# Gates multiplied into the experts' outputs instead of their inputs, and token rows stored unscaled

## The chip, the cores and the metric

The kernel runs on one core of a Trainium2 chip. The metric is the time of one execution in microseconds of the device, median of several runs. Engines are TensorE (PE; PEld for its weight loads), VectorE (DVE), ScalarE (ACT), GpSimd (POOL) and SyncE (SP), whose queue issues most of the transfers.

## The reference

Three computations follow one another. The first is a linear attention over 4 batches, 8 heads, 768 steps and heads of 48, in float32:

```
state = alpha_t[:, None] * state + k_t v_t^T        # per batch and head
y_t   = q_t state
```

The 3072 tokens of 384 features that come out go to a mixture of 8 experts, one expert per token:

```
logits = (x / (|x| + 1e-6)) @ (emb / (|emb| + 1e-6)).T / tau
e      = argmax(logits);  gate = softmax(logits)[e]
out    = gate * (relu(x @ w1[e]) @ w2[e])            # 384 -> 1024 -> 384
```

A dense block ends it: `h = x @ w_in` (2048 wide), `g = h if h > 0 else exp(min(h, 0)) - 1`, `g @ w_out`.

## The kernel before

**Attention and router.** The 3072 tokens are 24 tiles of 128 (6 pieces of the sequence by 4 batches). A loop written out by hand, `fast()`, goes through them one tile per iteration, and an `ending()` takes the last two; inside, the order of instructions on each engine is the order of the text (a manual schedule). For tile i, VectorE scans the decays (`stR`, L354, and `stA`, L364), GpSimd multiplies keys and queries by them (`Kh` L357, `Qh` L366), TensorE makes the scores psS (L394), VectorE masks them (L401), TensorE makes the outputs psY (L421, L439) and the state update, and one more TensorE product, psX (L476), gives the token rows, head by head in their final order, and the router's logits. `stD` copies the rows from PSUM (L493) and sums their squares (L495).

**Router groups.** Tiles are taken in groups, `GROUPS` (L38): 0–5, 6–11, 12–15, 16–19, 20–21, 22–23. When a group's last tile is done, `stR1` (L523 and following, VectorE) picks the expert of every token, `stR2` counts on TensorE (L572 to L576) where each token comes in its expert's region, and `stX` and `gates` make the gate. Of expert e the region in DRAM is `xs[e*REG:]`.

**Putting rows.** `scale_x` (L587) multiplies a tile's rows by their gates on ScalarE (L594) and splits the 32-bit words into two 16-bit planes (L601 on ScalarE, L603 on VectorE or GpSimd). `put` (L614, L615) adds the token's number and scatters the 128 rows to `xs` by an indirect DMA, issued by GpSimd. A DMA transpose (L263) brings an expert's rows back with features on the partitions, and `join` (L277 ScalarE, L279 GpSimd or VectorE) makes 32-bit words of the two planes again.

**Expert 0 starts before its last rows are stored.** Tiles 20 to 23 do not wait for the scatter and the transpose: `column` (L899) makes for each of them a matrix, gate where a token's place equals the column and zero elsewhere, and fp32 matmuls (L912) bring the rows to their columns in PSUM; three more (L938) add the joined rows of the other tiles by an identity matrix.

**Experts.** `moe1` goes through 8 experts of at most `CAPS` tokens, 432 down to 368. Every fp32 product is made of three fp32r passes, of high and low parts: `mm1` (L1064 to L1066), Relu and split (L1068 ScalarE, L1069 VectorE), `mm2` one or more blocks later (L1094 to L1096). Beside it, the weights of later experts are loaded by SP and split (L191 ScalarE, L194 VectorE); weights of the dense block are rounded by L229 to L235 on three engines; the next expert's rows are joined on GpSimd at f-step f−2 and split (`turn`, L1084 ScalarE, L1085 VectorE) at f−4. At the end of an expert its three output blocks go from PSUM to `x2T` (L1101, L1103 on ScalarE, L1102 on VectorE). `moe2` is the dense block; it writes the token's rows back by indirect DMA.

**Startup.** SP issues the loads of the first tiles, then `cs` (L709, the constants, among them `tok`, the tokens' numbers, and `base`), then more tiles. GpSimd's order there is: masks and zeros, the memsets of `vt` (L718), `Kh` and `Qh` of tile 0, of tile 1, the memsets of `G`. Twenty warm-up matmuls on TensorE stand ahead of the first psS:

```
                warm(ps1, "psY", 20)
                nc.vector.memset(pz[:, 0:1], A_FLOOR)
                nc.vector.memset(cum[:, 0], 0.0)
                for t in vt:
                    nc.gpsimd.memset(t[:, NP * CW:], 0.0)
                zero = xp.tile([128, 1, XW], U16, tag="xt", name="zero")
                for j in range(2):
                    stR(j); stA(j); stH(j); stE(j)
```

Of the kernel before, what the change touches and what calls it, by code (L numbers as in the profile page):

```python
# [8 lines left out]
F32 = mybir.dt.float32  # L9
# [28 lines left out]
GROUPS = [list(range(6)), list(range(6, 12)), list(range(12, 16)), list(range(16, 20)), [20, 21], [22, 23]]  # L38
NMID = 9
# [3 lines left out]
LOWS = (15, 18)  # L43
PAIRS = (15, 18, 19)
# [8 lines left out]
XW = 2 * (DM + 1)  # L53
# [14 lines left out]
def fused_kernel(ctx, tc, qk, a, v, w12, wi, wo, cst, cols, out):  # L68
# [9 lines left out]
    idl = dram.tile([N + CAP, 2], U16, name="idl")  # L78

# [9 lines left out]
    ident16 = const.tile([128, 128], BF16, name="ident16")  # L89
    base16 = const.tile([128, 1, E], BF16, name="base16")  # L90
# [5 lines left out]
    idf = const.tile([128, NT], F32, name="idf")  # L96
# [13 lines left out]
    tick = const.tile([1, 1], F32, name="tick")  # L110

# [161 lines left out]
    def join(eng, t, planes, kk, n):  # L273

        dst, src = words(t[:, :n]), planes[:, 2 * kk:2 * kk + 2, :n]
# [11 lines left out]
    def attention():  # L287
        with ExitStack() as st:
# [4 lines left out]
            xp = st.enter_context(tc.tile_pool(name="xp", bufs=14))  # L293
# [80 lines left out]
            def stT(i):  # L374
                if i < NT - B:
                    t = ps1.tile([128, NP, C2], F32, name="psT")
# [92 lines left out]
            def stD(i, keep=False):  # L469
# [13 lines left out]
                if keep:  # L483
                    late.pop()()
                rows = x[:, :, :CW]
                xi = xp.tile([128, XW], U16, name="xt")
                x3 = xi[:, :2 * DM].bitcast(F32).rearrange("p (n d) -> p n d", n=NP)
                sq = wk.tile([128, NP, CW], BF16, bufs=1, tag="junk", name="sq")
                if keep:
                    px[i] = x3  # L490
                else:
                    xt[i] = xi
                    nc.scalar.activation(out=x3, in_=rows, func=AF.Copy)  # L493
                    rows = x3
                nc.scalar.activation(out=sq, in_=rows, func=AF.Square, accum_out=ss[:, i:i + 1])  # L495
                if keep:
                    nc.scalar.activation(out=x3, in_=rows, func=AF.Copy)
# [51 lines left out]
            def gates(g):  # L549
                gt = gate[g]  # L550
                return [
                    lambda: nc.vector.tensor_scalar(gt, gt, 1e-9, None, op0=ALU.add),
                    lambda: nc.vector.reciprocal(gt, gt),
                ]

            def count_tile(g):
# [5 lines left out]
                if g == NG - 2:  # L562
                    return ps1.tile([128, 8, E], F32, tag="psT", name="psR")
                return psD.tile([128, 8, E], F32, tag="psX", name="psR")

            def stR2(g):
# [5 lines left out]
                nc.tensor.matmul(r, ident16, base16.to_broadcast(s3), start=True, stop=False)  # L572
                nc.tensor.matmul(r, ones16, cum[:, g:g + 1].to_broadcast(s3), start=False, stop=False)
# [12 lines left out]
            scaled = {}  # L586

# [802 lines left out]
```

## Time and profile before

| | us |
|---|---|
| median of 3 runs (780.39 to 780.43) | 780.4 |
| the profiled execution | 781.37 |
| its span in the trace | 779.7 |
| TensorE busy in the span | 759.2 (97%) |
| VectorE, ScalarE, GpSimd busy | 543.7, 355.1, 243.1 |
| mean granted clock of TensorE, of full | 0.988 |

The span runs from the first recorded instruction to the last; the execution's own time has 1.7 us more around it. A row of the timeline gives start and length of an instruction (or of several alike, with their count), its engine and line, what it writes from what, and in brackets how long the engine was idle before it and what it then waited for. A row of the windows gives for one stretch the busy time of every engine with the number of its instructions, the granted clock of TensorE as a share of 2.4 GHz, and the use of the DMA engines.

### The profile page before, as it was taken

The numbers are of one execution on the slowest core, as the hardware profiler recorded it, in microseconds if no ns is written. First come the engines' busy times: TensorE is split into PE (matmuls) and PEld (weight loads), VectorE is DVE, ScalarE is ACT, GpSimd is POOL, SyncE is SP. The second block draws the span as 40 slices with busy tenths as digits, with TensorE's granted clock in tenths as the row PEclk, the third lists the DMA queues.
The fourth block names the chain that finished last, engine by engine and source line by source line (L and its number), as shares of the span: only waits on it lengthen the run. The fifth ranks groups of instructions, "written<-read, shape, count | busy, mean of one in ns | idle before, by whom it ended". The sixth has DMA issues, their size and how long they took to land.

```text
span 779.7 us, 13453 instructions
## 1 busy us (share of the span) xinstructions
PE 759.2 (97%) x4982; PEld 689.5 (88%) x4982; DVE 543.7 (70%) x976; ACT 355.1 (46%) x698; POOL 243.1 (31%) x298
## 2 busy tenths in 40 slices
PE   8999998899999999999999999999999999999996
PEld 4888887489999999999887999999999999999996
DVE  7898998648999999995767745455454545545442
ACT  2557886635455555554545433333332333333331
POOL 7758787433565566451000020020010002002002
PEclk9999998899999999999999999999999999999998
DMA  9999952547757776751000010010000001001001
GB/s 194 249 258 254 253 155 75 164 119 187 216 188 215 234 205 211 216 181 32 1 1 1 0 42 1 1 41 0 1 11 31 0 1 42 1 0 42 1 1 41
DMA packets 59652, 75.31 MB, mean 97 GB/s; under 512 B 31134, under 2 KB 36126, under 8 KB 59582
## 3 DMA queue, kind: packets, MB, share of 16 engines
q1 hardware_dynamic: 56510, 64.97, 31.3%
q0 software_dynamic: 3072, 9.45, 3.4%
q8 instruction: 39, 0.64, 0.4%
q14 instruction: 31, 0.25, 0.1%
HBM read 57.20 MB, written 12.22 MB: 89 GB/s over the span
## 4 chain that ended last, share of the span: by engine, by line
issue 32%; PE 32%; DVE 8%; POOL 3%; ACT 3%; DMA 1%; POOLq 0%; ACTq 0%; SPq 0%; DVEq 0%
PE h L1243 6%; PE y L1095 3%; PE h L1065 3%; PE h L1066 3%; PE y L1096 3%; PE h L1064 3%; PE y L1094 3%; POOL out_dram L1277 2%; PE o L1266 2%; PE o L1264 2%; PE o L1265 2%; DVE wlo L194 2%; DVE dlo L250 1%; DVE hl L1069 1%; DVE g L1249 1%
## 5 line engine op out<-in xcount | busy, mean ns | idle before, releaser
L1245 DVE TENSOR_SCALAR mn<-h 128x512 f32<-128x512 f32 x96 | 66.3, 690 | 139.6 <-PE h L1243 139.6
L1246 ACT ACTIVATE mn<-mn 128x512 f32<-128x512 f32 x96 | 60.8, 633 | 171.6 <-DVE mn L1245 171.6
L1266 PE MATMUL o<-dwo,gl 128*128 128x384 f32 x384 | 129.6, 338 | 1.6 <-DVE gl L1253 1.6
L1265 PE MATMUL o<-dlo,gh 128*128 128x384 f32 x384 | 128.4, 334 | 0.0
L1277 POOL DMA_INDIRECT out_dram<-ob,ids x24 | 23.7, 988 | 335.5 <-ACT ob L1274 331.9
L1264 PE MATMUL o<-dwo,gh 128*128 128x384 f32 x384 | 128.3, 334 | 0.0
L1243 PE MATMUL h<-xh,dlo 128*128 128x512 f32 x288 | 113.1, 393 | 0.0
L1243 PE MATMUL h<-xl,dwi 128*128 128x512 f32 x288 | 112.9, 392 | 0.0
L1243 PE MATMUL h<-xh,dwi 128*128 128x512 f32 x288 | 112.7, 391 | 0.0
L1252 ACT ACTIVATE gh<-g 128x512 fp32r<-128x512 f32 x96 | 60.7, 633 | 77.6 <-DVE g L1249 77.6
L194 DVE TENSOR_TENSOR wlo<-raw,whi 128x512 fp32r<-128x512 f32 x96 | 88.1, 942 | 1.3 <-ACT whi L191 1.2
L1249 DVE SCALAR_TENSOR_TENSOR g<-mn,h 128x512 f32<-128x512 f32 x96 | 66.1, 689 | 15.3 <-ACT mn L1246 14.9
L1264 PEld LDWEIGHTS o<-dwo,gh 128*128 128x128 f32 x384 | 72.0, 187 | 4.2
L1265 PEld LDWEIGHTS o<-dlo,gh 128*128 128x128 f32 x384 | 72.0, 187 | 4.0
L1266 PEld LDWEIGHTS o<-dwo,gl 128*128 128x128 f32 x384 | 72.2, 188 | 2.7 <-DVE gl L1253 2.0
L1068 ACT ACTIVATE hh<-h 128x432 fp32r<-128x432 f32 (+6 forms) x64 | 32.4, 506 | 81.4 <-PE h L1066 76.8
L1095 PE MATMUL y<-hl,whi 128*128 128x432 f32 (+6 forms) x192 | 66.8, 348 | 1.4 <-DVE hl L1069 1.4
L1064 PE MATMUL h<-xh,whi 128*128 128x432 f32 (+6 forms) x192 | 66.5, 347 | 0.7 <-ACTq L1113 0.7
L1065 PE MATMUL h<-xl,whi 128*128 128x432 f32 (+6 forms) x192 | 66.4, 346 | 0.2 <-DVEq L1113 0.2
L1253 DVE TENSOR_TENSOR gl<-g,gh 128x512 fp32r<-128x512 f32 x96 | 65.6, 684 | 1.1 <-ACT gh L1252 1.1
L1066 PE MATMUL h<-xh,wlo 128*128 128x432 f32 (+6 forms) x192 | 66.4, 346 | 0.0
L1094 PE MATMUL y<-hh,whi 128*128 128x432 f32 (+6 forms) x192 | 66.3, 346 | 0.0
(228 smaller groups left out, 1484.5 us busy)
## 6 DMA issues: line engine op xcount, KB each, us to landing
raw<-in_w_dram SPq DMA_DIRECT2D x96, 256.0 KB, 3.4
qk<-in_qk_dram SPq DMA_DIRECT2D x46, 192.0 KB, 5.7
raw<-in_wi_dram SPq DMA_DIRECT2D x16, 384.0 KB, 3.9
raw<-in_wo_dram SPq DMA_DIRECT2D x16, 384.0 KB, 3.8
vt<-in_v_dram SPq DMA_DIRECT2D x24, 192.0 KB, 5.8
at<-in_alpha_dram SPq DMA_DIRECT2D x40, 99.0 KB, 5.8
xs<-zero SPq DMA_DIRECT2D x7, 288.8 KB, 5.9
at<-in_alpha_dram SPq DMA_DIRECT2D x4, 231.0 KB, 4.7
```

The costliest lines, as they stand in the source:

```text
L194: nc.vector.tensor_tensor(l[:, sl], r, h[:, sl].bitcast(F32), op=ALU.subtract)
L1064: nc.tensor.matmul(ps, wh, xh[:, kk], start=(kk == 0), stop=False)
L1065: nc.tensor.matmul(ps, wh, xl[:, kk], start=False, stop=False)
L1066: nc.tensor.matmul(ps, wl, xh[:, kk], start=False, stop=(kk == KD - 1))
L1094: nc.tensor.matmul(acc[e][d], wh, hh, start=(f == 0), stop=False)
L1095: nc.tensor.matmul(acc[e][d], wh, hl, start=False, stop=False)
L1243: nc.tensor.matmul(ps, l, x, start=(n == 0), stop=(n == len(terms) - 1))
L1245: nc.vector.tensor_scalar(mn, ps, 0.0, None, op0=ALU.min)
L1249: nc.vector.scalar_tensor_tensor(g, mn, -1.0, ps, op0=ALU.add, op1=ALU.max)
L1264: nc.tensor.matmul(o_, gh[:, sl], wh, start=(f == 0), stop=False)
L1265: nc.tensor.matmul(o_, gh[:, sl], wl, start=False, stop=False)
L1266: nc.tensor.matmul(o_, gl[:, sl], wh, start=False, stop=(f == M - 1))
```

## The change

- The rows are stored without the gate. ScalarE makes the two planes straight from psX in PSUM; `scale_x` is gone. A plane now holds all 384 features (`join` and the transposed tile follow), and a row has two more words of 16 bits for its gate.
- `mark` holds the token's number and the gate of every token. A GpSimd copy at the startup fills the numbers from `cs`; `gates` writes the gates, and `put` copies both into the row.
- Each expert's gates are read from `xs` by three small SP loads (`load_g`) to a row that is the same on all partitions, and VectorE multiplies the three output blocks by it. All three evictions are VectorE's.
- Groups become 0–5, 6–11, 12–15, 16–17, 18–21, 22–23. Tiles 18 to 23 go to expert 0 by columns of 0 and 1, with their rows split into two fp32r parts (`high` by ScalarE, `low` by VectorE); 36 fp32r matmuls stand for 12 fp32 ones (24 records).
- The transpose of expert 0's rows is issued behind the put of tile 17. Its joins are one on ScalarE and two on GpSimd; the other experts' joins are on ScalarE, one f-step later than before, and so is `turn`.
- `pack` and the tests of the decays are cut into pieces that go between the first splits and matmuls of expert 0; the branch on their result is read inside the second `mm1`. `stR2` starts from `cum`, which now holds the regions' bases, so that one matmul is gone.

The core of the diff:

```diff
-GROUPS = [list(range(6)), list(range(6, 12)), list(range(12, 16)), list(range(16, 20)), [20, 21], [22, 23]]
+GROUPS = [list(range(6)), list(range(6, 12)), list(range(12, 16)), [16, 17], list(range(18, 22)), [22, 23]]
+HOT = 18
-LOWS = (15, 18)
-PAIRS = (15, 18, 19)
+LOWS = (14, 15, 16)
+PAIRS = (15, 17, 19)
-XW = 2 * (DM + 1)
+XW = 2 * (DM + 2)
...
+    mark = const.tile([128, NT, 2], F32, name="mark")
...
                 warm(ps1, "psY", 20)
+                nc.gpsimd.tensor_copy(mark[:, :, 0], c["tok"])
                 nc.vector.memset(pz[:, 0:1], A_FLOOR)
-                nc.vector.memset(cum[:, 0], 0.0)
...
-                    nc.scalar.activation(out=x3, in_=rows, func=AF.Copy)
+                def planes():
+                    nc.scalar.activation(out=xt[i][:, :2 * DM].rearrange("p (two n d) -> p two n d", two=2, n=NP),
+                                         in_=x.bitcast(U16)[:, :, :2 * CW].rearrange("p n (d two) -> p two n d", two=2), func=AF.Copy)
                 nc.scalar.activation(out=sq, in_=rows, func=AF.Square, accum_out=ss[:, i:i + 1])
+                if pz is not None and i >= HOT:
...
+                    nc.scalar.activation(out=h, in_=rows, func=AF.Copy)
+                    late.append(lambda: nc.vector.tensor_tensor(l, rows, h.bitcast(F32), op=ALU.subtract))
+                if not hold:
+                    planes()
...
-                    lambda: nc.vector.reciprocal(gt, gt),
+                    lambda: nc.vector.reciprocal(mark[:, i0:i0 + n, 1:2].rearrange("p n o -> p (n o)"), gt),
...
-                nc.gpsimd.tensor_copy(x[:, 2 * DM:].bitcast(F32), c["tok"][:, i:i + 1])
+                x = xt.pop(i)
+                nc.gpsimd.tensor_copy(x[:, 2 * DM:].bitcast(F32), mark[:, i])
...
-                    nc.vector.tensor_scalar(hot[j], num, pos[:, j:j + 1], gate[g][:, b:b + 1], op0=ALU.is_equal, op1=ALU.mult)
+                    hot[j] = wk.tile([128, CAP], F32R, tag=tag, bufs=n, name="hot")
+                    nc.vector.tensor_scalar(hot[j], num, pos[:, j:j + 1], None, op0=ALU.is_equal)
...
+                    for j in tiles:
+                        for n, t in enumerate(px[j]):
+                            nc.tensor.matmul(t0[kk], t[:, kk * 128:(kk + 1) * 128], hot[j], start=(start and j == GROUPS[g3][0] and n == 0),
+                                             stop=(stop and j == tiles[-1] and n == 1))
...
-                    join(nc.gpsimd, xj[e, kk], xr[e], kk, CAPS[e])
+                    join(nc.scalar, xj[e, kk], xr[e], kk, CAPS[e])
...
+            def load_g(e, f):
+                if f == (0 if e else EARLY):
+                    gl[e] = xj_p.tile([1, CAP], F32, tag="xj", name="gl")
+                    nc.sync.dma_start(out=gl[e][:, :CAPS[e]].rearrange("o (n u) -> o n u", u=1),
+                                      in_=xs[bass.ds(expert(e) * REG, CAPS[e]), 2 * DM + 2:].bitcast(F32).rearrange("(o n) u -> o n u", o=1))
+                if f == (2 if e else EARLY + 1):
+                    nc.sync.dma_start(out=gd[e:e + 1, :CAPS[e]], in_=gl.pop(e)[:, :CAPS[e]])
+                if f == (4 if e else 5):
+                    gs[e] = gs_p.tile([128, CAP], F32, name="gs")
+                    nc.sync.dma_start(out=gs[e][:, :CAPS[e]], in_=gd[e:e + 1, :CAPS[e]].to_broadcast([128, CAPS[e]]))
...
-                    nc.scalar.activation(out=x2T[:, 0, bass.ds(o1, n)], in_=y[0], func=AF.Copy)
-                    nc.vector.tensor_copy(x2T[:, 1, bass.ds(o2, n)], y[1])
-                    nc.scalar.activation(out=x2T[:, 2, bass.ds(o1, n)], in_=y[2], func=AF.Copy)
+                    for d in range(KD):
+                        nc.vector.tensor_tensor(x2T[:, d, bass.ds(o, n)], y[d], gt[:, :n], op=ALU.mult)
...
-                        joined(e + 1, f - 2)
-                        turn(e + 1, f - 4)
+                        joined(e + 1, f - 3)
+                        turn(e + 1, f - 5)
+                        load_g(e, f)
```

## Rows read from the trace of the kernel before

**Rows 1.** Stages in one windows answer (us, PE, PEld, DVE, ACT, POOL busy, PEclk, DMA, GB/s).
```profile
35.68:111.14 75.46, 75.46 (x1116) 67.27 (x1114) 70.64 (x163) 53.01 (x121) 55.47 (x73) 1.00 0.96 243
...
122.27:129.37 7.10, 7.10 (x57) 6.03 (x57) 6.96 (x15) 1.56 (x6) 6.26 (x10) 0.55 0.33 90
...
129.37:156.68 27.31, 23.59 (x155) 15.43 (x154) 18.62 (x106) 19.05 (x44) 13.60 (x22) 0.87 0.44 139
...
156.68:371.84 215.16, 212.85 (x1152) 207.50 (x1152) 187.57 (x283) 112.01 (x227) 105.38 (x88) 1.00 0.62 181
```

**Rows 2.** Timeline of the startup, 0 to 14 us (start, us, engine, line, tiles, [idle before <-releaser]).
```profile
3.71 0.89 SPq L336 DMA_DIRECT2D qk<-in_qk_dram  x2
...
5.73 1.26 POOL L357 TENSOR_TENSOR Kh<-qk,R 112x512 f32<-112x512 f32 x1 [1.50 <-DVE R L354]
...
6.52 0.42 SPq L709 DMA_DIRECT2D cs<-in_cst_dram  x1
...
8.56 0.33 SPq L327 DMA_DIRECT2D at<-in_alpha_dram  x1
...
8.80 1.16 PE L394 MATMUL psS<-Qh,Kh 48*128 48x128 f32 x16
...
10.16 1.29 POOL L357 TENSOR_TENSOR Kh<-qk,R 112x512 f32<-112x512 f32 x1 [1.52 <-DMA qk<-in_qk_dram]
...
12.73 1.16 PE L394 MATMUL psS<-Qh,Kh 48*128 48x128 f32 x16 [0.93 <-POOL Qh L366]
```

**Rows 3.** Timeline of the first iterations, 13.5 to 40 us.
```profile
16.33 1.25 DVE L354 TENSOR_TENSOR_SCAN R<-at,pz 112x528 f32<-112x528 f32 x1 [0.79 <-DMA at<-in_alpha_dram]
...
17.20 1.16 PE L394 MATMUL psS<-Qh,Kh 48*128 48x128 f32 x16 [0.55 <-POOL Qh L366]
...
30.34 1.16 PE L394 MATMUL psS<-Qh,Kh 48*128 48x128 f32 x16 [0.36 <-POOL Qh L366]
```

**Rows 4.** DMA issues of the whole span (xcount, KB each, median us from issue to landing).
```profile
qk<-in_qk_dram SPq DMA_DIRECT2D x4, 96.0 KB, 3.2
...
idl<-xs SPq DMA_DIRECT2D x2, 1.7 KB, 7.6
```

**Rows 5.** Timeline of the loop's last iterations, 108 to 125 us.
```profile
117.25 1.24 DVE L354 TENSOR_TENSOR_SCAN R<-at,pz 112x528 f32<-112x528 f32 x1
...
122.27 1.40 PE L394 MATMUL psS<-Qh,Kh 48*128 48x128 f32 x16 [1.87 <-POOL Qh L366]
```

**Rows 6.** VectorE's lines between 84.8 and 126 us (xcount | busy us, mean ns | idle before).
```profile
L603 DVE COPY xt<-sx 128x768 uint16<-128x768 uint16 x3 | 2.8, 936 | 0.0
...
L523 DVE TENSOR_TENSOR lg<-lg,en 128x32 f32<-128x32 f32 x1 | 1.4, 1364 | 0.0
```

**Rows 7.** Timeline of the ending, first half.
```profile
140.62 2.04 PE L476 MATMUL psX<-rhsX,yT 128*128 128x104 f32 x8 [1.69 <-ACT yT L441]
```

**Rows 8.** Timeline of the ending, second half, 142 to 165 us.
```profile
146.60 0.92 DVE L899 TENSOR_SCALAR hot<-num,pos,gt 128x432 f32<-128x432 f32 x2
...
150.08 4.62 PE L912 MATMUL t<-hot,xt 128*128 128x432 f32 x12
...
154.53 2.34 PE L938 MATMUL t<-xj,masks 128*128 128x432 f32 x6
```

**Rows 9.** Stages of single experts, the first and the third (columns as in rows 1).
```profile
161.90:190.20 28.30, 28.30 (x144) 27.07 (x145) 17.03 (x26) 12.15 (x24) 8.04 (x8) 1.00 0.72 176
...
218.00:245.00 27.00, 27.00 (x145) 26.70 (x144) 26.63 (x40) 14.89 (x31) 16.23 (x13) 1.00 0.73 223
```

**Rows 10.** Waits between 162 and 372 us (us in total, times, longest).
```profile
PEld y L1095 <- DVE hl L1069: 3.1, 5, 1.0
```

**Rows 11.** VectorE's weight subtract (L194) and output copy (L1102), 156.7 to 371.8 us.
```profile
L194 DVE TENSOR_TENSOR wlo<-raw,whi 128x512 fp32r<-128x512 f32 x87 | 81.9, 967 | 1.3 <-ACT whi L191 1.2
...
L1102 DVE COPY x2T<-y 128x432 f32 x2 | 1.2, 599 | 0.6 <-PE y L1096 0.6
```

**Rows 12.** The weight subtract between 129.4 and 156.6 us.
```profile
L194 DVE TENSOR_TENSOR wlo<-raw,whi 128x512 fp32r<-128x512 f32 x3 | 1.9, 673 | 0.0
```

More of the change, by code (lines that the diff above doesn't have):

```diff
@@ L467, in attention, with stD @@
             px = {}
[L469 removed]
+            def stD(i, soon=False, hold=False):
                 if i < 0 or i >= NT:
@@ L889, in ending @@
-                run(r2, x2 + gates(g2))
-                xr = xr_p.tile([128, 2 * KD, CAP], U16, name="xr")
-                load_rows(xr, 0, [0, KD], puts[:-1])
-                stD(i, True)
-                hot = {}
-                def column(j, tag):
-                    g, b = place[j]
-                    hot[j] = wk.tile([128, CAP], F32, tag=tag, bufs=3 if tag == "Qh" else 2, name="hot")
-                    nc.vector.tensor_scalar(hot[j], num, pos[:, j:j + 1], gate[g][:, b:b + 1], op0=ALU.is_equal, op1=ALU.mult)
@@ new lines, in ending @@
+                for j, tag in zip(GROUPS[g3], ("Kt", "Kt", "A", "A")):
+                    column(j, tag, 2)
+                run(gates(g3))
+                last = [stD(i, True, True), stD(i + 1, True, True)]
+                m1, n1 = stR1(g1)
+                t0 = [psT_p.tile([128, CAP], F32, tag="psT", name="t0")] + [psG.tile([128, CAP], F32, tag="g", name="t0") for _ in range(KD - 1)]
+                n1.pop(0)()
+                run(m1)
+                for j in GROUPS[g3][:2]:
+                    put(j)
@@ new lines, in ending @@
+                pk = pack(sm, pz[:, 192:192 + E])
+                pk.pop(0)()
+                first_x(GROUPS[g3][2:], 1)
+                first_x(GROUPS[g3], 2, True)
+                run(r1)
+                for j in GROUPS[g1]:
+                    column(j, "Kh", 2)
+                xj = []
+                for kk, eng in enumerate((nc.scalar, nc.gpsimd, nc.gpsimd)):
+                    xj.append(xj_p.tile([128, CAP], F32, tag="xj", name="xj"))
+                    join(eng, xj[kk], xr, kk, CAP)
@@ new lines, in ending @@
+                for j in GROUPS[g3][2:]:
+                    put(j)
+                run(late)
+                late.clear()
+                run(n1, dec[7:11])
+                for kk in range(KD):
+                    nc.tensor.matmul(t0[kk], c["ident"], xj[kk], start=False, stop=False)
+                run(dec[11:13])
+                for kk in range(KD):
+                    first_x(GROUPS[g1], kk, stop=True)
+                for f in last:
+                    f()
+                x1 = stX(g1)
@@ new lines, in ending, with rest_of @@
+                tests = pk[:9] + dec[13:] + pk[9:]
+                tests, rest = tests[:len(tests) - 9], tests[len(tests) - 9:]
+                run(tests[:12])
+                tests = tests[12:]
+                def rest_of(n=None):
+                    if n is not None:
+                        run(tests[:n])
+                        del tests[:n]
+                        return
+                    run(tests, x1 + gates(g1))
+                    run(rest)
+                    for j in GROUPS[g1]:
+                        put(j)
+                    load_w(2 * PIECES)
+                    split_spare(len(spare))
@@ L961, in fix @@
                             general()
-                            run(pack(sm, ps1))
+                            run(pack(sm, psT_p.tile([128, E], F32, tag="psT", name="n_ps")))
                     zero = xp.tile([128, XW], U16, tag="xt", name="zero")
```

250 lines of the change are left out of this document (91 added, 159 removed).

## The prediction

> **What bounds the kernel now.** I read the stages first, then the order of work in the stages that the change touches, then the waits of the expert stage. The stages split into two kinds. Where TensorE is full, only its own work or its clock can move the time: from 35.68 to 111.14 us it is busy 75.46 of 75.46 us, and between 156.68 and 371.84 us, the experts, 212.85 of 215.16 us [rows 1]. Where it isn't full, chains of small instructions decide: the startup, until the first psS at 8.80 us [rows 2]; the last two loop iterations, where psS waits 1.87 us for GpSimd's Qh and the granted clock is then 0.55 for 7.10 us [rows 1, 5]; and the ending, from psS of tile 23 at 129.37 to the first expert matmul at 156.68, 27.31 us with 23.59 busy [rows 1]. The dense second product behind 371.84 us is not changed but for which rows it stores, and I cost it at nothing: TensorE sets its pace and its stores are issued by GpSimd beside it.
>
> The sum is made against the profiled execution, 781.37 us (span 779.7 and 1.7 around it). The median of the runs, 780.4, is 0.97 below, and I take that off at the end. About 0.2%, 1.56 us, is what a measurement here can tell from no change.
>
> **Startup: the copy of the token ids.** One GpSimd copy, mark from c["tok"], now stands before the memsets of vt and so before the first Kh. It reads cs, whose load SP issues only at 6.52 us, as the last of the first tiles' loads; before, nothing on GpSimd read cs so early, and the first Kh started at 5.73 [rows 2]. GpSimd works in the order written: what is queued behind the copy is Kh and Qh of tiles 0 and 1 and the memsets of G, and psS(0) waits for these. So the question is when cs lands, which no row shows. Two loads issued around it have their landing in a consumer's wait: the qk pair begun at 3.71 (its second part issued at about 4.15) lets Kh go at 10.16, 6.0 us later [rows 2]; alpha, issued at 8.56, lets the scan go at 16.33, 7.7 us later [rows 2, 3]. The bounds are 3.2 us, the fastest median of a load here [rows 4], and 7.7. Both neighbours in SP's queue are far from the fast end, so I go by them: 7.4 us, landing at 13.9. Then the copy (0.2), the memsets (0.3) and a handover put Kh(0) at 14.6 instead of 5.73, 8.9 later. The handover to A (Qh waited 0.2 for it) is gone, and psS(0) comes at about 17.15 instead of 8.80: +8.3.
>
> TensorE's warm-up matmuls still end at 8.9, so it stands idle 8 us. In this trace an idle stretch of 1.87 us was followed by matmuls at the 1.2 GHz level (0.55) [rows 1, 5], so psS(0), psT(0) and the six warm-ups, 3.2 us of work, begin slow: up to 3.2, I take +1.8. Against that, data and VectorE's scans are now ahead, and three waits of the next iterations for Qh can shrink: 0.93, 0.55 and 0.36 [rows 2, 3], together −1.84. From 35 us on the loop is TensorE's alone, so nothing gives the delay back later. Startup: **+8.3**, bounds +7 and +9.5 with cs at 13.9, and +4 with cs at 9.7.
>
> **The loop.** ScalarE loses a copy (0.49) and the scaling (0.60); under a full TensorE that is worth 0. The planes now read psX, which so stays held about 1.4 us instead of 0.5; two buffers at one tile per 5.3 us cover that, and without the cover it would cost the 0.9 per tile. What counts is VectorE near the end of the loop, because its scan R releases Kh, Qh and so psS; R(22) at 117.25 and the late Qh make the 1.87 us wait [rows 5]. Removed from VectorE there: three L603 copies, 2.8 us [rows 6]. Added: the router chain of the new group 16–17, about 2.7 us (the four-tile chain with its 1.36 us [rows 6] stall behind GpSimd was about 3.7 with that stall), low subtracts at 0.6 to 0.7 each for the hot tiles 18 to 20, two to three of them before R(23). Net +1.3 to +1.9 on VectorE, so R(22) near 119, psS(22) near 123.2, psS(23) near 130.3 by a clock that falls as before. **+0.9**, from +1.5 down to −2 if the wait gets short enough for the clock to stay at 2.4 GHz (7.10 us at 0.55 would then be some 3 shorter, less the added work).
>
> **The ending.** Before, two things follow the last tile. (a) Between the last fp32 hot columns, ready at 147.52 (146.60 + 0.92), and the first expert matmul at 156.68 lie 9.2 us: TensorE starts the last 12 records only at 150.08, behind tests of the pack, runs them 4.62 us, then the six of the joined rows, then an eviction [rows 8]. After, the joined rows (six records at 0.36, 2.2 us) go ahead of the last group. Of the 36 fp32r matmuls, at 0.197 us each (28.30 us / 144 [rows 9]) 7.1 us in all, 24 go beside the router chain, and 12 follow the last columns: 2.4 us, and 1.4 for splitting t0 (ScalarE and VectorE, from 155.25, the first third of L938's run, to 156.68). With a handover 4.7 instead of 9.2: −4.5, bounds −3.2 (the joins come last and their 2.2 us stand behind) and −5.7. The transpose of the rows is issued right behind the put of tile 17 instead of behind that of tile 19; before, it was not last either. (b) The last columns come earlier. The last psX starts at 140.62, 1.69 us late for yT, which ScalarE does behind the scaling and planes of the puts [rows 7]; these scalings are gone, and the psX could go at 138.9 or some 2 us sooner. But a four-tile router chain now lies between, with four columns of 0.46 us (half of 0.92 [rows 8]) on VectorE, 3.7 + 0.5 + 1.8 behind tile 21's logits at 132 (129.37 + 1.4 for psS [rows 5] + 1.1), so columns of 22 and 23 come at about 144.5 instead of 147.5: −3.1, bounds −1.3 and −3.9. Ending: **−7.6**, bounds −4.5 and −9.6. The added low subtracts here stand on VectorE beside TensorE's hot matmuls; uncovered they would take 0.7 each.
>
> **The experts.** Joins go from GpSimd to ScalarE: three per expert at 1.2 us; ScalarE has 14.89 busy of 27.00 us per expert and covers them [rows 9]. One copy and two ScalarE evictions become three VectorE multiplies; nearest row 0.60 [rows 11], so +1.2 us on VectorE, which is at 26.63 of 27.00 in the third expert [rows 9]. But the weight subtract takes 0.967 there [rows 11] and 0.673 where GpSimd does less [rows 12]; with 4.5 us of GpSimd's joins gone I expect some 2.4 us of VectorE back per expert. Net −1.2 a turn, and the 3.1 us in which weight loads wait for hl [rows 10] shrink. Joined and split one f-step later (3.3 us) than before, xl must be ready 1.5 to 2.8 us sooner than it is; that eats part. The three small loads of the gates stand on SP's queue: the second waits for the first, whose likeness lands in 7.6 us [rows 4], two steps of 3.3 us later, so SP may hold the weight loads behind it for about 1 us. I take **−0.5**, bounds −2.3 (all idle of the stage [rows 1]) and +4.
>
> **Sum:** 8.3 + 0.9 − 7.6 − 0.5 = +1.1; 781.37 + 1.1 = 782.5 in a profiled execution, 781.5 as a median.
>
> **The Trainium skill.** "DMA: Bandwidth & Descriptors", section "Anatomy of one DMA — SWDGE (gpsimd) path", fits a DMA's time as 2.0 us and its bytes over 436e3 per us; it is stated for another queue than SP's. For cs (48.5 KB) that is an estimate of 2.1 us: landed at 8.6. The 6.0 and 7.7 us of the loads around it [rows 2, 3] speak against it here.
>
> **Rivals.**
> R1, cs lands early. If a small load is served as fast as the fastest row, 3.2 us [rows 4], it lands at 9.7, Kh(0) goes at 10.4, and the startup loses 4 instead of 8.3: 777. Against it: both neighbours took twice that. 0.07. The Trainium skill's page "DMA: Bandwidth & Descriptors" stands on this side (8.6 by its fit, a startup of +3.4, an estimate of 776.6).
> R2, the copy holds nothing up, because GpSimd gets it late or something else bounds the startup: 781.5 − 8.3 = 773. Against it: nothing but psS(0)'s own chain starts the loop. 0.08.
> R3, the ending and the loop's end gain their better ends: the clock stays high (−2 for +0.9), ending −9.6: 781.5 − 2.9 − 2 = 777 or so. For it: half of the 27.31 us is waiting for single instructions. 0.17.
> R4, slower: VectorE becomes the bound of the experts. It has 0.4 us of slack in the third expert [rows 9]; if GpSimd's relief is not felt in L194, +1.2 puts it 0.8 over TensorE, and five such experts make +4 in place of −0.5: 786. It decides as soon as VectorE's expert exceeds TensorE's 27.0. 0.20.
>
> **Numbers.** The forecast has 0.48 and a range of its own of 779 to 784. Within it I give 0.06 to faster than 778.84, 0.24 to within 0.2% and 0.18 to slower than 781.96. R1, R2 and nearly all of R3 are faster, R4 slower: faster 0.36, same 0.26, slower 0.38. The range of 775 to 787 takes in R4 and R1, and leaves out R2 and the tails.
>
> **What would show it.** Startup: Kh(0) at 14 to 15 us, idle before it named as DMA cs, psS(0) near 17, a lower granted clock behind it. Loop: psS(23) minus psS(0) about 0.9 more than 120.57. Ending: from psS(23) to the first expert matmul about 20 us. Experts: L194's mean near 0.8 and no wait for hl; if it stays at 0.97 and TensorE waits for xl or hl, R4. I am wrong if Kh(0) starts before 11, or if the ending keeps over 24 us.

## The result: 790.8 us, slower by 1.3%

The changed kernel takes 790.79 us (median of 4 runs, 789.64 to 791.82) against 780.41 of the kernel before: ratio 1.0129, interval 1.0111 to 1.0146. That is above the range of 775 to 787. The profiled execution took 791.82 us, its span 789.8, at a granted clock of 0.989. By stages, each from the first matmul of one to the first of the next:

| stage | before, us | after, us | difference | predicted |
|---|---|---|---|---|
| start to psS(6) | 35.68 | 44.29 | +8.61 | +8.3 |
| psS(6) to psS(23) | 93.69 | 94.38 | +0.69 | +0.9 |
| psS(23) to the first expert matmul | 27.31 | 21.79 | −5.52 | −7.6 |
| experts | 215.33 | 221.35 | +6.02 | −0.5 |
| dense block to the end | 407.65 | 408.02 | +0.37 | 0 |
| sum | 779.66 | 789.83 | +10.17 | +1.1 |

A stage is read from one profiled execution, and the same code does not always take the same time in it. The loop and the ending, which `after` and `gl_own` (below) have word for word alike, took 94.38 and 21.79 us in the one and 92.72 and 21.27 in the other. So a difference of 2 us in these two stages proves little without a row that shows where it lies.

The startup of after, in its timeline; it answers to [rows 2]:
```profile
6.51 0.42 SPq L687 DMA_DIRECT2D cs<-in_cst_dram  x1
...
13.94 0.20 POOL L693 COPY mark<-cs 128x24 f32<-128x24 f32 x1 [10.07 <-DMA cs<-in_cst_dram]
14.34 1.25 POOL L356 TENSOR_TENSOR Kh<-qk,R 112x512 f32<-112x512 f32 x1
...
16.87 2.08 PE L393 MATMUL psS<-Qh,Kh 48*128 48x128 f32 x16 [7.79 <-POOL Qh L365]
...
21.76 1.16 PE L393 MATMUL psS<-Qh,Kh 48*128 48x128 f32 x16
```
GpSimd stands idle for 10 us in front of a copy of 0.20, and TensorE 7.8 behind it. The first psS, after that idle stretch, takes 2.08 us, the second 1.16.

The loop of after, psS(18) and psS(22) in its timeline, and the last 7 us before psS(23) in its windows; it answers to [rows 1, 5]:
```profile
109.89 1.16 PE L393 MATMUL psS<-Qh,Kh 48*128 48x128 f32 x16 [1.01 <-POOL Qh L365]
...
132.18 1.16 PE L393 MATMUL psS<-Qh,Kh 48*128 48x128 f32 x16 [1.85 <-POOL Qh L365]
```
```profile
131.67:138.67 7.00, 6.49 (x56) 5.52 (x57) 5.48 (x14) 1.66 (x4) 6.24 (x11) 0.65 0.38 129
```
The wait in front of psS(22) is the one of the kernel before (1.87). New is the one in front of psS(18), which comes 6.41 us behind psS(17), 5.34 in the kernel before.

The ending of after, in its timeline; it answers to [rows 8]:
```profile
138.67 2.04 PE L393 MATMUL psS<-Qh,Kh 48*128 48x128 f32 x16
...
148.24 1.50 DVE L853 TENSOR_SCALAR hot<-num,pos 128x432 fp32r<-128x432 f32 x4
...
152.62 3.46 DVE L853 TENSOR_SCALAR hot<-num,pos 128x432 fp32r<-128x432 f32 x2
...
153.26 2.23 POOL L278 COPY xj<-xr 128x864 uint16<-128x864 uint16 x2
```
Four columns take 1.50 us; the two that start 0.64 us ahead of GpSimd's joins take 3.46 and end 0.59 us after them (156.08 against 155.49).

The experts of after: the stage, and one expert in its middle (windows, columns as in [rows 1, 9]), then the waits of the stage (total us, times, longest; [rows 10]), then VectorE's weight subtract ([rows 11]):
```profile
160.46:381.81 221.35, 213.74 (x1154) 207.23 (x1152) 183.06 (x318) 125.04 (x234) 78.11 (x68) 1.00 0.65 187
...
249.00:275.50 26.50, 26.50 (x146) 26.48 (x145) 23.68 (x41) 16.80 (x32) 11.91 (x10) 1.00 0.72 212
```
```profile
DVE xl L1075 <- ACT xh L1074: 5.9, 6, 3.1
PE h L1053 <- DVE xl L1075: 5.3, 4, 2.0
...
ACT xj L276 <- DMA gd<-gl: 3.6, 1, 3.6
...
PEld y L1085 <- DVE hl L1059: 1.0, 2, 0.7
```
```profile
L193 DVE TENSOR_TENSOR wlo<-raw,whi 128x512 fp32r<-128x512 f32 x89 | 68.9, 801 | 9.5 <-ACT whi L190 9.5
```
TensorE is idle for 7.6 us here (221.35 − 213.74) against 2.3 before, and 5.3 of it are four waits for xl (1.28, 1.14, 0.82 and 2.03 us). VectorE, which makes xl, itself waits 5.9 us there for ScalarE's xh. VectorE is not full: 23.68 of 26.50 us in this expert, its subtract down from 967 to 801 ns.

### The profile page after: what moved, and what is told of

The parts are those of the page before. It is cut to its first block, busy times and chain, and to the rows that moved or that the text cites. A ratio compares the mean times of both kernels' runs of the same rounds, so it can differ in the third digit from the quotient of the medians.

```text
span 789.8 us, 13493 instructions
## 1 busy us (share of the span) xinstructions
PE 758.2 (96%) x4988; PEld 690.8 (87%) x4988; DVE 538.1 (68%) x995; ACT 345.6 (44%) x665; POOL 213.9 (27%) x277
## 4 chain that ended last, share of the span: by engine, by line
issue 32%; PE 30%; DVE 8%; ACT 3%; POOL 2%; DMA 2%; POOLq 0%; SPq 0%; ACTq 0%; DVEq 0%
PE h L1241 6%; PE h L1053 3%; PE h L1054 3%; PE y L1085 3%; PE y L1084 3%; PE y L1086 3%; PE h L1052 3%; PE o L1264 2%; PE o L1262 2%; PE o L1263 2%; POOL out_dram L1275 2%; DVE wlo L193 2%; DVE dlo L249 1%; DVE xl L1075 1%; DVE hl L1059 1%
## 5 line engine op out<-in xcount | busy, mean ns | idle before, releaser
L193 DVE TENSOR_TENSOR wlo<-raw,whi 128x512 fp32r<-128x512 f32 x96 | 76.1, 817 | 9.5 <-ACT whi L190 9.5
```

What stands on the lines that cost most here:

```text
L193: nc.vector.tensor_tensor(l[:, sl], r, h[:, sl].bitcast(F32), op=ALU.subtract)
```

## The experiments

**The startup from both sides.** before_copy adds one line to the kernel before, at the place where the change has its copy; copy_late moves the copy in after behind GpSimd's startup work.
```diff
  (before_copy)
                 warm(ps1, "psY", 20)
+                nc.gpsimd.tensor_copy(pos, c["tok"])
  (copy_late)
                 warm(ps1, "psY", 20)
-                nc.gpsimd.tensor_copy(mark[:, :, 0], c["tok"])
...
                 nc.gpsimd.memset(ones_f, 1.0)
+                nc.gpsimd.tensor_copy(mark[:, :, 0], c["tok"])
```


> The kernel before with one GpSimd copy added: the token numbers from cs into pos (overwritten later), between the warm-up matmuls and the memsets of vt, where the change has its copy of them. One part of the change alone. Theory (startup): Kh(0) at 14.3 us, psS(0) at 17, the loop runs at TensorE's pace and keeps all of it: +8.3, 788.7. Rival (the loop's own waits, 2.2 us for Qh, and those of the ending take part of the delay up): +6 or less, 786.

> The changed kernel with one line moved: the GpSimd copy of the token numbers into mark stands behind the memsets of G, zero and ones_f instead of ahead of the memsets of vt. Theory (startup): the copy's wait for cs holds Kh(0) and so psS(0); moved, Kh(0) goes at 5.7 us as before, psS(0) at 8.8, and the whole comes out 8 us shorter, about 782.5. By then cs has landed (13.94 us) or nearly, so the copy waits for little. Rival (something else in the new startup, such as the DMA order, sets the pace): psS(0) stays later than 12 us and the gain is under 4 us, 787 or more. The experts stay at about 221 us from first expert matmul to the dense block by both.


before_copy: 790.03 us, ratio 1.0119 [1.0104, 1.0133]. psS(0) goes at 17.22 us, psS(6) at 44.50, 8.82 later than before. Behind it the loop gives back 1.10 us (92.59, at a granted clock of 1.00 against 0.97), and ending and experts take 1.5 more than before. From its timeline:
```profile
14.30 0.20 POOL L715 COPY pos<-cs 128x24 f32<-128x24 f32 x1 [10.42 <-DMA cs<-in_cst_dram]
```
So one copy of 0.2 us, alone, costs 9.5 us (790.03 against 780.54), nearly the whole net change; the rest of the change comes out near zero beside it. copy_late: 785.31, ratio 1.0054 [1.0034, 1.0074]. psS(6) comes at 35.54, 8.75 earlier than in after, but the time falls by 5.5 only: the loop takes 97.32 instead of 94.38 and the experts 222.64. From copy_late's timeline:
```profile
8.36 1.16 PE L393 MATMUL psS<-Qh,Kh 48*128 48x128 f32 x16
...
57.72 0.61 SPq L601 DMA_DIRECT2D xs<-zero  x1
...
64.43 1.18 POOL L593 DMA_INDIRECT xs<-xt,pos_i  x1 [3.65 <-DMA raw<-in_w_dram]
...
69.06 1.16 PE L393 MATMUL psS<-Qh,Kh 48*128 48x128 f32 x16 [1.19 <-POOL Qh L365]
```
The first put, one iteration earlier than in the kernel before, waits 3.65 us for a transfer (I read it as the last zero fill, issued at 57.72; the profile names another that ended then), and Kh and Qh stand behind it. In after the late startup hid this: its puts come 8 us later. The wait costs 2 of the loop's 2.9 us: from psS(6) to psS(17) copy_late takes 61.14 us, after 59.19, and best2 (below), which has that put one iteration later, 59.19 again. The other 0.9 lie behind psS(18), where the granted clock over the last 7 us is 0.53 in copy_late and 0.65 in after.

**When the next expert's rows are ready.** Four kernels cross two edits of after: the steps at which joins and turn run, and the engine of the joins; a third edit gives the gates' first load a buffer of its own.
```diff
  (turn_early; turn_early_gl and pool_early_gl too)
-                        joined(e + 1, f - 3)
-                        turn(e + 1, f - 5)
+                        joined(e + 1, f - 2)
+                        turn(e + 1, f - 4)
  (joins_pool; pool_early_gl too)
-                    join(nc.scalar, xj[e, kk], xr[e], kk, CAPS[e])
+                    join(nc.gpsimd, xj[e, kk], xr[e], kk, CAPS[e])
  (gl_own; turn_early_gl and pool_early_gl too)
-                    gl[e] = xj_p.tile([1, CAP], F32, tag="xj", name="gl")
+                    gl[e] = pos[:, 4 * (e % 6):4 * (e % 6) + 4]
...
```


> The changed kernel with joins and splits of the next expert's rows put back one f-step, joined at f-2 and turn at f-4, as before the change; joins stay on ScalarE, the gates' first tile still shares the joins' buffers. Theory (late turn): xl of the next expert is late because its last third is split in the last f-step; one step of 3.3 us earlier removes the waits for xl, 5 to 6 us, and the experts take 215 to 217 us instead of 221: 785 to 786 in all. Rival (joins on ScalarE hold hh): waits move to hh, the experts stay over 219 us. Rival (shared buffer): a join now has to wait for the gate row's store, which it reuses, and ScalarE's wait for gd<-gl grows over 3.6 us in sum.

> As turn_early, and the gates' first tile is 108 by 4 in a small tile of its own (pos, which is idle then) instead of a join's buffer. Theory (late turn, with the shared buffer as a second wait): no ScalarE wait for gd<-gl, no xl waits, experts at 215 us, 784.5 in all. If the shared buffer costs nothing: as turn_early within 1 us. If joins on ScalarE are the cause: over 219 us for the experts as well.

> The changed kernel with the joins of experts 1 to 7 back on GpSimd, at the late steps (joined f-3, turn f-5). Theory (late turn): xl stays late, the experts stay at 220 us or more, and the weight subtract on VectorE is slow again (mean 0.95 instead of 0.82): 790 to 794. Rival (joins on ScalarE): the joins no longer stand ahead of hh and xh on ScalarE, the waits go, experts at 216 us, 785.

> The changed kernel, joins and splits at its own late steps, with the gates' first tile in a place of its own (108 by 4 in pos) instead of a join's buffer. Theory (two separate causes in the experts: the late turn and the shared buffer): ScalarE's wait for gd<-gl, 3.6 us, and the waits for hh and hl near 188 us go, 1.6 us, the waits for xl at the later experts stay, 4 us; experts 219 to 220 us, 789.2. If the late turn alone is the cause: 221 as before.

> The changed kernel with joins on GpSimd, at the steps of the kernel before (f-2, f-4), and the gates' first tile in its own place: the experts as before the change but for the multiplies on VectorE and the gates' loads. Theory (late turn and shared buffer are the whole cause): experts at 215 to 217 us, like before (215.3), 785. Rival (VectorE is then over-full, since GpSimd's joins slow its subtracts and the multiplies add 1.2 us per expert): experts at 219 us or more, waits for hl and xl in every expert.

| kernel | turn | joins | gl | median, us | ratio | experts, us | TensorE idle in them, us | its waits for xl: number, us |
|---|---|---|---|---|---|---|---|---|
| after | f−5 | ScalarE | shared | 790.79 | 1.0129 | 221.35 | 7.6 | 4, 5.3 |
| turn_early | f−4 | ScalarE | shared | 793.98 | 1.0158 [1.0126, 1.0189] | 223.37 | 7.3 | none |
| turn_early_gl | f−4 | ScalarE | own | 789.10 | 1.0107 [1.0084, 1.0129] | 217.63 | 3.9 | none |
| joins_pool | f−5 | GpSimd | shared | 794.85 | 1.0178 [1.0140, 1.0216] | 224.71 | 10.2 | 4, 4.3 |
| gl_own | f−5 | ScalarE | own | 792.88 | 1.0170 [1.0153, 1.0187] | 223.42 | 7.9 | 4, 4.2 |
| pool_early_gl | f−4 | GpSimd | own | 797.55 | 1.0217 [1.0200, 1.0234] | 228.80 | 10.4 | none |

Idle is the stage less TensorE's busy time. Where the granted clock falls, a stage grows by more than its idle time: in gl_own the clock is 0.72 between 355 and 360 us, in turn_early 0.50 between 190 and 195, each behind an idle stretch of TensorE; in after it is 1.00 throughout the experts.

The waits of turn_early's experts, then one of joins_pool's and its weight subtract:
```profile
ACT xj L276 <- DMA gd<-gl: 5.0, 1, 5.0
...
ACT xj L276 <- DMA xr<-xs: 6.3, 1, 6.3
...
PEld y L1084 <- ACT hh L1058: 4.8, 2, 3.0
```
```profile
PE h L1053 <- DVE xl L1075: 4.3, 4, 2.0
```
```profile
L193 DVE TENSOR_TENSOR wlo<-raw,whi 128x512 fp32r<-128x512 f32 x89 | 78.1, 903 | 0.0
```
The waits for xl go with the step of the turn, on either engine of the joins. gl_own and turn_early_gl differ by these steps alone: TensorE's idle time falls from 7.9 to 3.9 us, the kernel's from 792.88 to 789.10. But with the shared buffer earlier joins gain nothing, because another wait takes the place of the first: a join on ScalarE that waits for a transfer holds hh, which is queued behind it on the same engine. Of the two transfers, gd<-gl holds the join because the gates' first load took one of the joins' three buffers; with a buffer of its own (turn_early_gl) the stage is 3.7 us shorter than in after, and what is left is the join's 6.0 us wait for xr and 2.3 for gs. gl_own was expected at 789 and missed: with that buffer alone the xl waits remain (4.2 us) and the gates arrive 2.6 us late for the first multiply.

turn_early_gl and pool_early_gl differ by the engine of the joins alone: 789.10 against 797.55 us. So the joins belong on ScalarE, as the change has them. With them on GpSimd, rival R4 shows in part: the weight subtract takes 970 ns, VectorE is busy 26.82, 26.26 and 26.41 us in the stretches 222 to 250, 250 to 277 and 277 to 304, and TensorE waits six times for hl, 3.6 us in all. Two longer waits (4.8 us) are for x2T, behind gates that land 3.5 us late, so VectorE is not shown to be the bound of that stage.

**The ending.** end_act puts the ending's two GpSimd joins on ScalarE.
```diff
-                for kk, eng in enumerate((nc.scalar, nc.gpsimd, nc.gpsimd)):
+                for kk, eng in enumerate((nc.scalar, nc.scalar, nc.scalar)):
```


> The changed kernel with the three joins of expert 0 in the ending all on ScalarE (one there and two on GpSimd before). Theory (VectorE's second column of 22 and 23 is held while GpSimd joins: two columns took 3.46 us there, 0.92 before the change): the columns take about 1 us, the last matmuls start some 2.5 us earlier and from psS(23) to the first expert matmul come out 19.3 us instead of 21.8; 788.3 in all. Rival (the tests of the decays, VectorE's chain to the matmul of L814, set the time): the columns are short but the first expert matmul moves by less than 1 us.


789.70 us, ratio 1.0122 [1.0098, 1.0146], not to be told from after's 790.79; psS(23) to the first expert matmul falls from 21.79 to 19.74. From its timeline:
```profile
151.02 3.21 ACT L276 ACTIVATE xj<-xr 128x864 uint16<-128x864 uint16 x3
...
151.43 0.80 DVE L853 TENSOR_SCALAR hot<-num,pos 128x432 fp32r<-128x432 f32 x2
```
The same two columns take 0.80 us beside ScalarE's joins and 3.46 beside GpSimd's. It is the overlap that counts: gl_own has its joins where after has them, but there the columns come first:
```profile
150.71 0.79 DVE L853 TENSOR_SCALAR hot<-num,pos 128x432 fp32r<-128x432 f32 x2
...
153.06 2.21 POOL L278 COPY xj<-xr 128x864 uint16<-128x864 uint16 x2
```
What the short columns are worth in time is less sure. best2 and best6 (below), with the same joins, have 19.8 us in this stage too, but best3 has 22.46, at a granted clock of 0.79 against best2's 1.00, and pairs_sp 21.85, where psS(23) comes 2.7 us earlier than in best2 and the joins wait 2.1 us for their transfer.

**All of these together.** best2 has the late copy, the first put one iteration later, turn_early_gl, end_act, and for the second expert's rows joins at f−3. best3 also issues the gates' loads ahead of joins and turn. best3_evict lets ScalarE copy two of three output blocks and so leaves their gate out, to see what the multiplies cost.
```diff
  (best2)
-                    for j in [j for j in putq if place[j][0] in gated][:2 if i in PAIRS else 1]:
+                    for j in [j for j in putq if place[j][0] in gated and i > 10][:2 if i in PAIRS else 1]:
...
+                        joined(e + 1, f - (2 if e else 3))
+                        turn(e + 1, f - 4)
```


> All repairs together: token numbers copied late, first put one iteration later (i over 10, so that GpSimd doesn't wait for the last zero fill), joins and splits one f-step earlier on ScalarE (the first join of expert 1 stays late, so that it doesn't wait for its transpose), gates in their own place, the ending's joins on ScalarE. If the separate gains add: startup and loop -6.8 of the changed kernel's, ending -2.5, experts -4.5 to -6: 776 to 778, faster than both. If they don't add (the loop's own waits come back when the startup is short): 780 to 782.

> As best2, with the gates' loads issued ahead of the joins of the same f-step and so ahead of the next transpose on SP's queue. Theory (in best2 the gates of expert 0 came 2.7 us late because their last load stood behind the transpose of expert 2, which holds SP's queue for 8.6 us; VectorE's three multiplies and then TensorE's first mm2 of expert 1 waited for it): no wait of x2T for gs, TensorE's 2.3 us wait at the first boundary and the two or three waits behind it go: experts 216 to 217 us instead of 220.5, 776.5. Rival (the waits behind it have causes of their own): 219 us or more, 779.

> As best3, with two of the three output blocks copied by ScalarE without their gate and one multiplied by VectorE, as the evictions stood before the change; the gate of two thirds of the features is left out. Theory (three serial multiplies on VectorE, 1.6 us behind its queue, hold the accumulators that TensorE's next expert needs): the waits of mm2 for x2T go and the experts are 1 to 2 us shorter than in best3. Rival (evictions are covered): no difference within 0.5 us.


best2: 779.96, ratio 0.9995 [0.9977, 1.0013]; best3: 780.05, 0.9992 [0.9981, 1.0004]; best3_evict: 779.09, 0.9983 [0.9969, 0.9996], not to be told from best3, and its experts are not shorter (219.7 us against best3's 218.0). All of the loss is back, and no gain. The multiplies are not what is left. In best2 the experts still take 220.53, with the first gates late:
```profile
172.49 8.56 SPq L262 DMA_TRANSPOSE xr<-xs  x1
...
181.15 0.52 SPq L1040 DMA_DIRECT2D gs<-gd  x1
...
185.37 1.64 DVE L1091 TENSOR_TENSOR x2T<-y,gs 128x432 f32 x3 [2.71 <-DMA gs<-gd]
```
SP issues the gates' last load only after a transpose whose row takes 8.56 us. In best3 the wait for gs is gone and the experts take 218.0 us, 2.5 less, but the kernel's time is that of best2: 776.5 was expected.

**Two edits that changed nothing.** best5 has joins at f−3 for the third expert's rows too; best6 also moves a weight split from iteration 16 to 17 (`LOWS`), for a wait of 1.0 us at psS(18).
```diff
  (best5)
-                        joined(e + 1, f - (2 if e else 3))
+                        joined(e + 1, f - (2 if e > 1 else 3))
  (best6)
-LOWS = (14, 15, 16)
+LOWS = (14, 15, 17)
```


> As best3, with the first joins of expert 2 one f-step later too (f-3 for the joins of experts 1 and 2, f-2 for the others). Theory (what is left of the experts' loss is ScalarE's first join of expert 2, which waits 2.7 us for its transpose in front of hh, so that mm2 waits 1.2 to 2.3 us): no wait of a ScalarE join for xr, and the experts take 216 to 217 us instead of 218 to 219.7; 778.3. Rival (the delay sits in the weights' loads behind the transposes on SP's queue): 218 us or more, 780.

> As best5, with the third early split at iteration 17 instead of 16 (LOWS 14, 15, 17). Theory (the 1.0 us that TensorE loses before psS(18) comes from that one VectorE subtract, 2.6 us long beside GpSimd's Kh and Qh instead of 0.7): the step from psS(17) to psS(18) is 5.3 to 5.5 us instead of 6.4, 777.3. Rival (the changed order of the puts makes it): 6.4 us as before, same time as best5.


best5: 780.82, 1.0003 [0.9993, 1.0014], and the wait for hh that it was to take away stays. best6: 780.31, 0.9997 [0.9985, 1.0009], and psS(17) to psS(18) is 6.41 us as before it. Two rows of best6, the loop's wait and ScalarE's at the second expert:
```profile
101.11 1.16 PE L393 MATMUL psS<-Qh,Kh 48*128 48x128 f32 x16 [1.00 <-POOL Qh L365]
...
189.39 0.56 ACT L232 ACTIVATE dg<-raw 128x384 f32<-128x384 f32 x1 [6.23 <-DMA raw<-in_wi_dram]
```
The second row moved the question: hh waits there behind a rounding of dense weights that have not landed, not behind a join. For the first, the two puts of iteration 15 were left (scatters at 95.40 and 96.92, Kh behind them at 98.53); the next kernels have PAIRS = (17, 18, 19) instead of (15, 17, 19).

**The gates' loads.** gates_pool_q issues two of the three on GpSimd's queue; gates_pool_pairs has the later double puts as well; gates_dram makes one load of the first two, from DRAM to DRAM; pairs_sp leaves the loads as in best3; no_gates has no gate loads and multiplies by ones.
```diff
  (gates_pool_q)
-                    nc.sync.dma_start(out=gs[e][:, :CAPS[e]], in_=gd[e:e + 1, :CAPS[e]].to_broadcast([128, CAPS[e]]))
+                    nc.gpsimd.dma_start(out=gs[e][:, :CAPS[e]], in_=gd[e:e + 1, :CAPS[e]].to_broadcast([128, CAPS[e]]))
  (gates_pool_pairs, gates_dram, pairs_sp, no_gates)
-PAIRS = (15, 17, 19)
+PAIRS = (17, 18, 19)
  (gates_dram)
+                    nc.sync.dma_start(out=gd[e:e + 1, :CAPS[e]].rearrange("o (n u) -> o n u", u=1),
+                                      in_=xs[bass.ds(expert(e) * REG, CAPS[e]), 2 * DM + 2:].bitcast(F32).rearrange("(o n) u -> o n u", o=1))
  (no_gates)
+                    nc.gpsimd.memset(gs[e], 1.0)
```


> As best3, with the second and third load of each expert's gates (their store to DRAM and the load to all partitions) issued on GpSimd's queue instead of SP's; the first stays on SP's. Theory (SP's queue stands still while those loads wait for one another, so weights come late; ScalarE's decode waits 6.2 us for them at expert 1 in front of hh, and TensorE 2.2 us behind that): ScalarE's wait for weights near 185 us falls under 2 us, mm2 of expert 1 doesn't wait for hh, experts 216 to 217 us; 778. Rival (the transposes alone hold the queue): no change, 218 to 220 us, 780. Second rival: GpSimd waits for the landings itself and its decode comes late, seen as waits of VectorE or ScalarE for GpSimd.

> As gates_pool_q, with the double puts at iterations 17, 18 and 19 instead of 15, 17 and 19. Theory (the 1.0 us before psS(18) is GpSimd's: two puts in iteration 15, 3.4 us, in front of Kh and Qh): the step from psS(17) to psS(18) is 5.3 to 5.6 us; the loss may come back behind iteration 17 or 18, where psS already waits for Qh, so the whole gains 0 to 1 us over gates_pool_q.

> As best3, with the double puts at iterations 17, 18, 19 and with each expert's gates taken from xs to the small DRAM tensor by one load instead of two over on-chip memory. Theory (two causes left: the double put of iteration 15, 1.0 us, and SP's queue, which waits for the landing of the gates' first load before the second): psS(17) to psS(18) 5.33 us, SP's waits for the gates' store gone, weights of expert 1 earlier, experts 216 to 217.5 us; 777.5. Rival (the transposes hold SP's queue): only the loop's 1.0 or less, 779.3.

> As best3, with the double puts at iterations 17, 18, 19, gates loaded on SP's queue in three steps as in best3. Theory: the loop gains 0.5 to 1.0 us, experts as best3 at 218 to 220 us; 779.3. Rival (the experts' start takes the gain up, since their waits hang on transfers with times of their own): 780.

> As pairs_sp, with the gates' three loads per expert left out: the three blocks are multiplied by ones, made by a GpSimd memset of the same tile, so the output lacks the gates. Theory (the loads of the gates, of 4-byte pieces and in SP's queue ahead of the transposes and the weights, are what is left of the experts' loss; in gates_dram another form of them cost 23 us): weights come in time, ScalarE's decode waits for them about as before the change, mm2 of expert 1 doesn't wait for hh, experts 215 to 217 us instead of 220, and 775 to 776.5 in all. Rival (joins on ScalarE in front of hh, or the three multiplies): 218.5 us or more, 779.

| kernel | median, us | ratio | experts, us | psS(17) to psS(18), us |
|---|---|---|---|---|
| gates_pool_q | 788.67 | 1.0083 [1.0055, 1.0111] | 226.71 | |
| gates_pool_pairs | 784.76 | 1.0053 [1.0031, 1.0074] | 224.83 | 5.33 |
| gates_dram | 801.85 | 1.0277 [1.0254, 1.0300] | 242.99 | |
| pairs_sp | 779.78 | 0.9998 [0.9983, 1.0012] | 220.13 | 5.33 |
| no_gates | 774.33 | 0.9918 [0.9905, 0.9932] | 214.54 | |

The double put was the loop's wait: without it the step takes 5.33 instead of 6.38 (gates_pool_pairs against gates_pool_q). The whole time shows nothing of it where the loads are SP's: pairs_sp has 779.78, best3 780.05. GpSimd's queue is the worse place for the gates; a load stands there behind a wait of 13.1 us (gates_pool_q's waits in the experts; the profile names VectorE's wlo, and in gates_pool_pairs TensorE's h for a wait of 13.3, so what it waited for is open):
```profile
POOL gd L1037 <- DVE wlo L193: 13.1, 1, 13.1
...
PE y L1084 <- DVE x2T L1091: 8.9, 3, 7.0
```
The experts of pairs_sp and of no_gates (windows), and ScalarE's waits for the dense weights in pairs_sp, in no_gates and in gates_dram:
```profile
149.50:369.63 220.13, 214.88 (x1154) 208.52 (x1152) 182.52 (x318) 125.50 (x234) 77.10 (x68) 0.99 0.70 188
```
```profile
149.31:363.85 214.54, 212.96 (x1153) 207.19 (x1152) 183.19 (x318) 125.55 (x234) 81.34 (x76) 1.00 0.66 185
```
```profile
ACT dg L232 <- DMA raw<-in_wi_dram: 11.5, 5, 5.9
ACT dg L232 <- DMA raw<-in_wo_dram: 9.6, 8, 3.1
```
```profile
ACT dg L232 <- DMA raw<-in_wo_dram: 5.9, 8, 1.8
...
ACT dg L232 <- DMA raw<-in_wi_dram: 4.3, 3, 2.1
```
```profile
ACT dg L232 <- DMA raw<-in_wi_dram: 25.9, 8, 6.4
...
ACT dg L232 <- DMA raw<-in_wo_dram: 19.7, 7, 7.1
```
The two windows differ by the gates' loads (and eight GpSimd memsets in their place): the stage is 5.6 us shorter without them, 0.8 below that of the kernel before, with the same VectorE and ScalarE work. Of the 5.6 us TensorE's idle time makes 3.7; the other 1.9 are matmuls at a lower granted clock, 0.66 between 190 and 195 us in pairs_sp and 1.00 throughout in no_gates. best3, with the same loads and no such fall, is 3.5 above no_gates. So the joins on ScalarE and the three multiplies do fit, and the loads are what keeps the change from paying: they make the dense weights land late, ScalarE waits for these at their rounding, and hh behind it. Whether it is their place in SP's queue or their many 4-byte pieces (64941 DMA packets against 59650) was not separated. no_gates isn't a version to use; no complete one beat the kernel before by more than its interval.

## Why the prediction was wrong

**Right: the startup (+8.3, measured +8.61).** cs was put at 13.9 from the two loads around it, and the copy read it at 13.94; Kh(0) 14.6 against 14.34, psS(0) 17.15 against 16.87. The slow matmuls behind the idle stretch came too: the granted clock is 0.71 from 16.87 to 24.00 us. By the fit of the Trainium skill, "DMA: Bandwidth & Descriptors", "Anatomy of one DMA — SWDGE (gpsimd) path", which is given for GpSimd's queue, cs would be there at an estimated 8.6; the trace has 13.94, and the two loads around it told better. R1 and R2 are out (by the prediction's own steps, cs at 8.6 gives a startup of +3.0, not R1's +3.4; nothing hangs on it). before_copy shows the whole of this step alone.

**Right in number, not in mechanism: the loop (+0.9, +0.69).** The working had VectorE's added work make psS(22) late. The step from psS(21) to psS(22) is 6.20 us against 6.14 before, so that did not show. What came is 1.07 us in front of psS(18), from the two puts of iteration 15 (scatters at 104.20 and 105.72 us; in the kernel before two puts come one iteration later), which the working did not look at, 0.3 more up to psS(22), and 0.61 back from there to psS(23), at a granted clock of 0.65 against 0.55. That the sum fits is luck. With the startup mended, copy_late lost 2.9 us more here, 2.0 of them to a put that I had not looked at, because my sum had it 8 us late. The clock was to stay high if that wait got short enough; in gl_own the wait is as long as before and the clock stays high.

**Half right: the ending (−7.6, −5.52).** Term (a), from the last columns to the first expert matmul, was 9.16 us and is 4.38 (160.46 − 156.08): −4.8, predicted −4.5, though of other parts: 1.9 us up to the last twelve matmuls, behind VectorE's row tests, and 2.5 for these; the split of t0 (1.4 in the working) goes beside them. Term (b) had the last columns 3.1 earlier; counted from psS(23) they start as forecast but take 3.46 us and not 0.92, so they end 0.7 earlier. I took the duration from a row in which GpSimd did no 16-bit copies [rows 8]; in end_act the columns take 0.80 and the stage is 2.05 shorter, of the 2.1 that were missing; the kernel's time does not show it. R3's reason, that half of the 27.31 us is waiting, does not fit its row, where TensorE is busy 23.59.

**Wrong: the experts (−0.5, +6.02), and with them the forecast.** VectorE's relief was right: 967 to 801 ns, and the waits for hl fell from 3.1 us to 1.0 [rows 10, 11]. The failed step is "Joined and split one f-step later … that eats part". The working had xl 1.5 to 2.8 us too late and gave that no price of its own, but set it against VectorE's relief. It is not a matter of VectorE's load: xl is due at a fixed matmul, and issued 3.3 us later it misses that at four of seven boundaries, by 0.8 to 2.0 us, 5.3 in all. The stage's idle time rose by these 5.3 us (2.3 to 7.6). gl_own against turn_early_gl shows it, and joins_pool that the engine of the joins doesn't change it.

The second miss is the gates, "about 1 us" inside my bounds: their loads, in the form they have in best3 and pairs_sp, cost 3.5 and 5.6 us against no_gates. In after itself this is not seen: ScalarE waits 10.6 us for dense weights there, 16.1 in the kernel before, and 5.3 of TensorE's 7.6 idle us are the waits for xl. The loads' price shows once these are gone, so the two don't add. R4 named a time (786) for a mechanism that after does not have; pool_early_gl shows a part of it with the joins on GpSimd.

## What to carry to other kernels

Before a small instruction goes into an in-order queue, find when its operand lands: it costs everything behind it that wait, whatever its own length, and here 0.2 us of work cost 9.5. Price a moved step by the time at which its first consumer needs it, not by the load of the engine that does it. When a delay ahead is mended, look again at the waits that it covered. Give small loads that are issued among bulk loads a price of their own. And where a stage's time fits the sum, check that it went where the working had it.

## What was not expected of the hardware

- Two VectorE tensor_scalar of 128x432 take 0.80 us beside ScalarE, 0.92 in the kernel before [rows 8], 0.79 with two 16-bit copies on GpSimd 1.6 us behind them (gl_own), and 3.46 beside such copies.
- One DRAM-to-DRAM load of 4-byte pieces per expert in place of two loads through the on-chip buffer made the experts 22.9 us longer (242.99 against 220.13): the median landing of the first dense weights (`in_wi`) is 6.1 us there, 4.6 in no_gates and 3.9 in the kernel before.
- A DMA transpose's row on SP took 2.5 to 3.5 us in seven places and 8.56 in one (best2; 6.99 at most in the kernel before), and what SP issues next comes behind it.
- The same wait is not always followed by a lower clock. In after TensorE waits 1.85 us in front of psS(22), the granted clock over the last 7 us before psS(23) is 0.65, and psS(23) comes 6.49 us behind psS(22). In gl_own, which has the same loop, the wait is 1.87, the clock 1.00, and psS(23) comes 4.82 us behind:
```profile
130.63:137.63 7.00, 4.58 (x62) 3.71 (x59) 6.83 (x15) 3.01 (x7) 6.30 (x9) 1.00 0.20 64
```
